# Two raw quads moved into an idle MLP buffer, with a newly searched instruction order, in a hand-ordered attention and MLP kernel

## The chip, the cores and the metric

One core of a Trainium2 chip. The metric is the device time of one execution in microseconds (us), median over timed runs; the four timed runs of the kernel before spread over 0.4% (358.04 to 359.32). Each profile is one further execution with its trace. "Half clock" below is a granted TensorE clock of 0.50 in the trace.

## The reference

```python
def phi(x):                                   # q, k, v: (8 batch, 8 heads, 576, 64); omega: (128, 64)
    proj = np.einsum('bhsd,md->bhsm', x, omega)
    return np.concatenate([np.cos(proj), np.sin(proj)], axis=-1) / np.sqrt(m)
q_p, k_p = phi(q), phi(k)
kv = np.einsum('bhsm,bhsd->bhmd', k_p, v);  z = np.sum(k_p, axis=2)
num = np.einsum('bhsm,bhmd->bhsd', q_p, kv);  den = np.einsum('bhsm,bhm->bhs', q_p, z)
x = (num / den) as (8, 576, 512)              # den kept away from 0
h = x.transpose(0, 2, 1) @ U @ V              # rank 32
u = x + h.transpose(0, 2, 1)
out = u + np.maximum(u @ w_ch1, 0.0) @ w_ch2  # 512 -> 2048 -> 512
```

The features are sines and cosines of random projections, so attention needs no score matrix. All matmuls run in bf16 with float32 sums.

## The kernel before

Every instruction of the kernel is a named word with its needs and buffers, and one long string, `ORDER`, says in which order the words are issued. Each engine runs its own words in that order: before, POOL issued `ld/q/2` at 13.03 us and `ld/k/3` at 15.61. The string was found by a search. The words of the argument, where a group `g` is a pair of heads ("head" in the prediction and below) and a quad `n` is two groups:

- `ld/k/n`, `ld/q/n`: load of a quad's keys or queries, issued by POOL (GpSimd). `ldv/n`: of its values. `low`: of the low-rank matrices V and U; `gate` clears their buffer first.
- `tpp/k/n`, `tp/k/n`: PE's transposes of the loaded quad, and their copy out of PSUM by DVE (VectorE).
- `ak/g`, `aq/g`: projections of keys and queries (64-row matmuls). `uk/g`, `uq/g`: DVE turns them into integer angles, 1.48 us and 1.21 us each.
- `s/c` (and `sk sq ck cq`): sine and cosine on ACT (ScalarE). `p` (`pk pq`): the quarter turn between them, on POOL.
- `kv/g`, `kvb/g`, `num/g`, `x/g`: key-value product (64 rows), its copy by DVE, the numerator, the division by DVE.
- `hu ut0 hn`: low-rank mixing. `w1 r w2 o st`: the MLP. `d/i`: a filler matmul on the identity. `@n`: the PSUM bank.

```python
    low_f = hidp.tile([P, NFT, SM], BF16, name="hid").rearrange("p f t -> p (f t)").bitcast(F32)
    Vf = low_f[:, 0:S]                          # the second of two hidden buffers stages V and U at first
    ...
    NRAW = 2                                    # two raw buffers for the quads' keys and queries
    def load(name, n):
        if ("raw", n) not in held:
            held["raw", n] = rawp.tile([P, 2, 2, NS * D], BF16, name="raw")
        return held["raw", n][:, "kq".index(name), :, :]
    ...
    need = [r for r in read_raw(name, n - NRAW)] if n >= NRAW else []
    add(("ld", name, n), POOL, lambda ...: nc.gpsimd.dma_start(load(name, n), quad(src, n)), needs=need)
    ...
    if n in BY_PE:                              # quads 0 to 3: transposed by PE
        add(key, PE, lambda ...: tp(key, blocks), needs=src + old + ["ident"], ...)
        add(done, on, lambda ...: ev(key, blocks, on), needs=[key], frees=[key])
    ...
    add(("uk", g), DVE, uk, needs=[("ak", g)] + slot, frees=[("ak", g)])
    add(("uq", g), DVE, uq, needs=[("aq", g), ("uk", g) if g else ("ukh", 0, 0)], frees=[("aq", g)])
```

So the third quad (`n = 2`) may be loaded only when the first quad's transposes have left its raw buffer.

Of the kernel before, what the change touches and what calls it, by code (L numbers as in the profile page):

```python
# [20 lines left out]
R = 32  # L21
# [14 lines left out]
begin first/k/0 first/k/1 ident first/q/0 om ld/k/0 d/0@5 warm d/1@1 ld/q/0 d/2@0 ld/k/1 d/3@7 d/4@5 ld/q/1 d/5@0 cast/k/1 cast/k/0 d/6@2  # L36
ldv/0 omb d/7@0 tpp/k/0/0@3 tpp/k/0/1@4 omt@7 tp/k/0/0 cast/q/0 WT tpp/k/0/2@0 tp/k/0/1 akh/0/0@5 tp/k/0/2 tpp/q/0/0@7 tpp/q/0/1@1 ukh/0/0
ld/k/2 tp/q/0/0 akh/0/1@2 tp/q/0/1 ukh/0/1 aq/0@4 d/8@6 gate skh/0/0 uq/0 d/9@7 low ak/1@0 skh/0/1 at/0@3 d/10@6 ut/0 pk/0 tpp/k/1@6 uk/1
sq/0 tpp/q/1@4 ck/0 ldv/1 pq/0 tp/k/1 d/11@1 aq/1@1 tp/q/1 ld/q/2 cq/0 uq/1 ak/2@3 wv/0 aq/2@6 uk/2 d/12@1 s/1 W1/0 ldv/2 kv/0/0@0 ld/k/3
uq/2 ak/3@2 W1/1 kv/0/1 p/1 uk/3 s/2 aq/3@6 kvb/0 tpp/k/2@2 uq/3 tpp/q/2@4 c/1 p/2 num/0 tp/k/2 tp/q/2 d/13@2 sk/3 x/0 ak/4@5 ld/q/3 wv/1  # L40
kv/1/0@3 c/2 uk/4 kv/1/1 pk/3 aq/4@1 kvb/1 kv/2/0@6 uq/4 sq/3 kv/2/1 lowc num/1 ck/3 kvb/2 kv/3/0@1 x/1 num/2 pq/3 kv/3/1 ld/k/4 hu0/0@0
cq/3 kvb/3 ut0x/0@3 huc0/0 hu0/1@4 ld/q/4 x/2 ut0/0 s/4 ut0x/1@0 W1/2 d/14@5 num/3 huc0/1 W1/3 ute0/0 hu0/2@7 ut0x/2@4 ut0/1 huc0/2
w1p/0/0@3 x/3 p/4 ut0/2 ute0/1 tpp/k/3@5 ute0/2 w1p/2/0@0 w1p/2/1 tp/k/3 hu0/3@7 w1p/1/0@2 w1p/3/0@1 huc0/3 ak/5@4 wv/2 c/4 w1p/3/1 uk/5
w1p/1/1 w1p/1/2 ut0x/3@7 ut0/3 w1p/3/2 w1p/2/2 w1p/0/1 ute0h/3 w1p/0/2 tpp/q/3@4 ute0/3 tp/4 w1/0/0 tp/q/3 aq/5@6 r/0/0 w1/0/1 w1/0/2 uq/5
w1/0/3 r/0/1 hn/0/0@4 r/0/2 w1/0/4@3 u/0/0 r/0/3 ldv/3 w1/0/5@0 r/0/4 s/5 ak/6@4 aq/6@1 w1/0/6@3 uk/6 w1/0/7@7 r/0/5 p/5 uq/6 r/0/6
w1/0/8@5 r/0/7 ak/7@0 r/0/8 aq/7@3 s/6 kv/4/0@6 uk/7 W2/0 w1/0/9@5 W2/1 kv/4/1 uq/7 W2/2 w1/0/10@2 r/0/9 p/6 c/5 hn/0/1@0 kvb/4 w1/0/11@5
u/0/1 num/4 wv/3 r/0/10 w1/0/12@4 x/4 r/0/11 w1/0/13@0 W2/3 r/0/12 d/15@1 kv/5/0@5 r/0/13 kv/5/1 s/7 ak/8@0 kvb/5 aq/8@3 w2/0/0/0@7 uk/8
num/5 c/6 p/7 uq/8 w1/0/14@0 w2/0/0/1 x/5 r/0/14 kv/6/0@1 ld/k/5 kv/6/1 c/7 ak/9@3 ld/q/5 w1/0/15@0 uk/9 ld/k/6 hnt/0@6 w2/0/0/2 ld/q/6
r/0/15 kvb/6 ut/tail/0 s/8 kv/7/0@3 kv/7/1 aq/9@5 num/6 kvb/7 num/7 x/6 p/8 w2/0/0/3 x/7 w2/0/1/0@0 w2/0/1/1 o/0/0 c/8 uq/9 w2/0/1/2 tp/5
hu/1@1 w2/0/1/3 s/9 huc/1 w2/0/2/0@7 o/0/1 hn/1/0@5 ldv/4 w2/0/2/1 p/9 st/0/0 u/1/0 hn/1/1@0 w2/0/2/2 u/1/1 w2/0/2/3 c/9 tu/1 w2/0/3/0@0  # L50
o/0/2 ak/10@2 ak/11@5 uk/10 w2/0/3/1 wv/4 tp/6 w2/0/3/2 uk/11 aq/10@3 w2/0/3/3 uq/10 kv/8/0@6 ldv/5 kv/8/1 kv/9/0@1 st/0/1 s/10 kvb/8
aq/11@4 kv/9/1 num/8 kvb/9 st/0/2 uq/11 w1/1/0@3 ldv/6 p/10 num/9 x/8 r/1/0 w1/1/1@4 s/11 o/0/3 w1/1/2@5 x/9 ld/k/7 w1/1/3@6 r/1/1 wv/5
w1/1/4@7 r/1/2 r/1/3 hnt/1@2 p/11 w1/1/5@0 r/1/4 ut/tail/1 c/10 ak/12@4 w1/1/6@1 uk/12 ld/q/7 w1/1/7@2 r/1/5 ld/k/8 r/1/6 ak/13@5 ld/q/8
r/1/7 kv/10/0@3 uk/13 aq/12@0 c/11 kv/10/1 w1/1/8@2 uq/12 w1/1/9@7 r/1/8 aq/13@5 kvb/10 tp/7 kv/11/0@0 r/1/9 uq/13 kv/11/1 s/12 num/10
w1/1/10@2 kvb/11 x/10 num/11 s/13 p/12 w1/1/11@5 x/11 tp/8 w1/1/12@3 w1/1/13@6 r/1/10 wv/6 r/1/11 hu/2@1 r/1/12 w1/1/14@0 r/1/13 huc/2
ld/k/9 c/12 w1/1/15@2 ld/q/9 hn/2/0@6 p/13 w2/1/0/0@3 u/2/0 r/1/14 hn/2/1@4 r/1/15 w2/1/0/1 u/2/1 c/13 ak/14@0 aq/14@6 w2/1/0/2 tu/2 uk/14
w2/1/0/3 uq/14 w2/1/1/0@0 o/1/0 kv/12/0@1 ldv/7 s/14 kv/12/1 ldv/8 kv/13/0@6 kvb/12 ak/15@3 st/0/3 kv/13/1 num/12 kvb/13 uk/15 tp/9 p/14
num/13 w2/1/1/1 x/12 w2/1/1/2 c/14 w2/1/1/3 x/13 wv/7 aq/15@1 ak/16@3 o/1/1 w1/2/0@6 uq/15 ld/k/10 w1/2/1@7 r/2/0 uk/16 ak/17@0 r/2/1
w1/2/2@6 s/15 uk/17 w1/2/3@5 w1/2/4@3 r/2/2 p/15 w1/2/5@2 r/2/3 r/2/4 hnt/2@0 w1/2/6@5 r/2/5 ut/tail/2 ld/q/10 aq/16@3 r/2/6 aq/17@6
kv/14/0@1 wv/8 c/15 kv/14/1 w1/2/7@5 kvb/14 uq/16 ld/k/11 num/14 w2/1/2/0@0 uq/17 s/16 w1/2/8@3 x/14 w2/1/2/1 tp/10 r/2/7 p/16 w1/2/9@4  # L60
r/2/8 kv/15/0@1 r/2/9 ak/18@5 st/1/0 kv/15/1 uk/18 aq/18@3 c/16 w2/1/2/2 ldv/9 w2/1/2/3 ldv/10 kvb/15 st/1/1 num/15 s/17 w1/2/10@7 x/15
w2/1/3/0@5 uq/18 r/2/10 w1/2/11@1 o/1/2 kv/16/0@6 r/2/11 ak/19@2 kv/16/1 s/18 st/1/2 wv/9 uk/19 aq/19@0 w2/1/3/1 ldv/11 w2/1/3/2 uq/19
wv/10 w1/2/12@4 kvb/16 ld/q/11 hu/3@2 r/2/12 ld/k/12 num/16 huc/3 w2/1/3/3 p/17 x/16 w1/2/13@1 hn/3/0@2 r/2/13 p/18 w2/2/0/0@7 u/3/0 c/17
w1/2/14@6 w1/2/15@0 r/2/14 hnt/3@1 hn/3/1@2 r/2/15 w2/2/0/1 s/19 u/3/1 w2/2/0/2 o/1/3 w2/2/0/3 ut/tail/3 c/18 st/1/3 p/19 w2/2/1/0@5 o/2/0
ak/20@0 st/2/0 kv/17/0@6 uk/20 w2/2/1/1 ld/q/12 c/19 tu/3 aq/20@3 kv/17/1 uq/20 ak/21@0 w2/2/1/2 kvb/17 w2/2/1/3 uk/21 tp/11 num/17
w2/2/2/0@4 x/17 s/20 w2/2/2/1 tp/12 o/2/1 kv/18/0@0 kv/18/1 aq/21@6 p/20 kv/19/0@2 kvb/18 kv/19/1 num/18 kvb/19 st/2/1 uq/21 w2/2/2/2
w2/2/2/3 x/18 s/21 num/19 ld/k/13 w1/3/0@0 x/19 w1/3/1@1 p/21 r/3/0 o/2/2 w1/3/2@7 r/3/1 ak/22@3 r/3/2 aq/22@1 ld/q/13 w1/3/3@0 uk/22 c/20
ld/k/14 w2/2/3/0@7 uq/22 w2/2/3/1 r/3/3 c/21 kv/20/0@5 ak/23@0 aq/23@3 kv/20/1 uk/23 w2/2/3/2 tp/13 s/22 w2/2/3/3 kvb/20 w1/3/4@0 o/2/3
uq/23 num/20 ldv/12 p/22 r/3/4 st/2/2 w1/3/5@7 hu/4@1 r/3/5 st/2/3 w1/3/6@3 huc/4 s/23 x/20 w1/3/7@2 w1/3/8@0 r/3/6 p/23 hnt/4@6 r/3/7
w1/3/9@5 ut/tail/4 r/3/8 w1/3/10@3 r/3/9 w1/3/11@0 wv/11 r/3/10 c/22 hn/4/0@6 ld/q/14 hn/4/1@2 u/4/0 w1/3/12@1 ld/k/15 ld/q/15 w1/3/13@4  # L70
u/4/1 r/3/11 wv/12 r/3/12 w1/3/14@7 r/3/13 tu/4 w1/3/15@6 r/3/14 ak/24@3 r/3/15 ak/25@0 uk/24 c/23 w2/3/0/0@7 tp/14 w2/3/0/1 uk/25
w2/3/0/2 kv/21/0@5 kv/21/1 aq/24@0 ak/26@2 kvb/21 w2/3/0/3 uq/24 num/21 o/3/0 w2/3/1/0@0 x/21 st/3/0 w2/3/1/1 uk/26 w2/3/1/2 w1/4/0@1
w1/4/1@5 r/4/0 aq/25@6 r/4/1 kv/22/0@1 uq/25 kv/23/0@3 s/24 kv/22/1 kv/23/1 w1/4/2@5 kvb/22 kvb/23 num/22 p/24 num/23 x/22 s/25 w2/3/1/3
x/23 w1/4/3@6 r/4/2 w1/4/4@7 p/25 o/3/1 r/4/3 hu/5@4 c/24 st/3/1 w2/3/2/0@2 huc/5 w2/3/2/1 r/4/4 aq/26@0 kv/24/0@3 kv/24/1 ak/27@5 kvb/24
w2/3/2/2 uq/26 w2/3/2/3 uk/27 w1/4/5@0 w1/4/6@1 o/3/2 r/4/5 num/24 r/4/6 w1/4/7@0 c/25 x/24 hn/5/0@1 hn/5/1@5 u/5/0 w1/4/8@4 r/4/7
w1/4/9@7 u/5/1 r/4/8 w2/3/3/0@0 r/4/9 tu/5 s/26 w2/3/3/1 aq/27@1 kv/25/0@3 uq/27 kv/25/1 ak/28@5 p/26 w2/3/3/2 st/3/2 kvb/25 s/27 uk/28
w1/4/10@2 ldv/13 w1/4/11@1 ldv/14 r/4/10 w1/4/12@7 p/27 r/4/11 num/25 r/4/12 w2/3/3/3 x/25 w1/4/13@2 o/3/3 w1/4/14@4 r/4/13 wv/13 c/26
w1/4/15@3 w2/4/0/0@7 ldv/15 st/3/3 w2/4/0/1 r/4/14 r/4/15 aq/28@5 tp/15 kv/26/0@0 uq/28 ak/29@2 kv/26/1 w2/4/0/2 uk/29 s/28 w2/4/0/3
w2/4/1/0@6 o/4/0 c/27 kvb/26 w1/5/0@2 p/28 st/4/0 w2/4/1/1 w1/5/1@7 r/5/0 c/28 hnt/5@3 w2/4/1/2 ut/tail/5 w2/4/1/3 r/5/1 w2/4/2/0@3 o/4/1
w1/5/2@2 num/26 r/5/2 w1/5/3@7 x/26 w2/4/2/1 r/5/3 w2/4/2/2 kv/27/0@0 ak/30@4 kv/27/1 uk/30 w2/4/2/3 w1/5/4@2 o/4/2 w1/5/5@5 kvb/27 r/5/4  # L80
w1/5/6@4 r/5/5 num/27 r/5/6 aq/29@2 x/27 ak/31@4 w2/4/3/0@7 uq/29 w2/4/3/1 w1/5/7@1 uk/31 w1/5/8@2 r/5/7 w1/5/9@5 r/5/8 s/29 w1/5/10@6
w1/5/11@1 w2/4/3/2 r/5/9 p/29 r/5/10 hu/6@0 r/5/11 w2/4/3/3 w1/5/12@2 o/4/3 wv/14 huc/6 w1/5/13@6 r/5/12 c/29 hn/6/0@0 hn/6/1@4 u/6/0
w1/5/14@7 w2/5/0/0@2 u/6/1 r/5/13 r/5/14 w1/5/15@0 tu/6 w2/5/0/1 r/5/15 kv/28/0@6 aq/30@4 aq/31@0 kv/28/1 w2/5/0/2 kvb/28 st/4/1 uq/30
w2/5/0/3 st/4/2 uq/31 w2/5/1/0@3 s/30 w2/5/1/1 st/4/3 w2/5/1/2 p/30 w2/5/1/3 num/28 w2/5/2/0@0 x/28 c/30 w2/5/2/1 o/5/0 w1/6/0@7 o/5/1
st/5/0 s/31 w2/5/2/2 st/5/1 w1/6/1@2 w1/6/2@5 r/6/0 p/31 r/6/1 w1/6/3@1 w1/6/4@2 wv/15 c/31 w2/5/2/3 w1/6/5@4 o/5/2 w1/6/6@3 st/5/2 r/6/2
# [57 lines left out]
def kernel(  # L143
# [125 lines left out]
    def load(name, n):  # L269
        if ("raw", n) not in held:  # L270
            held["raw", n] = rawp.tile([P, 2, 2, NS * D], BF16, name="raw")
        return held["raw", n][:, "kq".index(name), :, :]
# [427 lines left out]
```

## Time and profile before

| | |
|---|---|
| time, median | 358.24 us (358.04 to 359.32 over all runs beside the changed kernel) |
| the profiled execution | 360.0 us (its span 358.0), so 1.8 us over the median |
| PE (matmuls) busy | 95% of the span |
| half clock | 14.8 to 25.1 us, then full to the end |
| first head's num begins | 23.13 us |
| fourth head's num begins (the prediction's "mark") | 31.89 us |

The line numbers of one place differ by up to 4 between kernels, as the buffer lines push them down: the transposes are L321 before, L325 after, L324 in most experiments. Read PE's share first: what the kernel takes is a nearly gapless row of matmuls, plus what PE loses in the first 32 us. The prediction below shows the lines for that. The timeline columns are start, length, engine, line, operation and tiles; those of the busy time of each engine are stretch, its length, then PE, PEld, DVE, ACT, POOL, then clock, DMA share, GB/s.

```profile
8.31 0.71 POOL L298 DMA_DIRECT2D raw<-in_k_dram  x1 [3.48 <-PE ps L407]
```

```profile
23.13:31.89 8.76, 7.70 (x213) 6.03 (x211) 7.84 (x16) 7.57 (x6) 6.26 (x10) 0.89 0.78 122
```

The third quad's k load was issued at 8.31 us. From the first num to the mark DVE worked 7.84 us of 8.76: already then the fullest row, just ahead of PE (7.70).

### The profile page before, as it was taken

The page shows a single profiled execution, that of the slowest core. Times are in us where ns is not written, and L with a number is a line of the kernel's source. Part 1 is how long each engine was busy: PE and PEld are TensorE (multiplying, and loading weights), DVE is VectorE, ACT ScalarE, POOL GpSimd, SP SyncE. Part 2 cuts the span into 40 slices and gives each one's busy share as a digit, 9 for nine tenths or more (in the row PEclk, how much of TensorE's full clock was granted, in tenths as well). Part 3 has the DMA queues.
Part 4 walks back from the last instruction along what each step waited for, and adds up shares of the span by engine and source line. Part 5 has one row for each costly group of instructions (what it writes and reads, how often), then busy time and mean ns, then how long its engine had stood idle before and what let it go on. Part 6 is the DMA issues. An engine that isn't in the chain of part 4 may idle for free.

```text
span 358.0 us, 8213 instructions
## 1 busy us (share of the span) xinstructions
PE 341.3 (95%) x3544; PEld 180.4 (50%) x3585; DVE 193.2 (54%) x284; ACT 216.8 (61%) x223; POOL 117.3 (33%) x100
## 2 busy tenths in 40 slices
PE   7659999999999999989999999999999999999996
PEld 3446456454564554645455554554545544444444
DVE  3968868786687676866476754364320722000111
ACT  5868899559958877678829578437386004553210
POOL 5879185427634536324704043003230000000000
PEclk9869999999999999999999999999999999999999
DMA  8997989999999886999992086200722051511124
GB/s 173 224 239 116 203 142 195 217 178 227 192 194 192 123 246 128 115 177 166 196 183 46 3 212 140 62 3 0 148 60 44 2 104 29 117 31 29 37 53 88
DMA packets 68567, 45.06 MB, mean 126 GB/s; under 512 B 47156, under 2 KB 59828, under 8 KB 68532
## 3 DMA queue, kind: packets, MB, share of 16 engines
q1 hardware_dynamic: 55348, 30.09, 41.2%
q0 software_dynamic: 12816, 13.93, 25.5%
q8 instruction: 28, 0.46, 0.5%
q10 hardware_dynamic: 368, 0.52, 0.4%
q14 instruction: 7, 0.06, 0.1%
HBM read 37.16 MB, written 9.44 MB: 130 GB/s over the span
## 4 chain that ended last, share of the span: by engine, by line
PE 88%; DMA 7%; ACT 1%; issue 1%; POOL 1%; POOLq 0%
PE ps L610 35%; PE ps L630 34%; PE ps L430 5%; PE ps L444 4%; DMA raw<-in_q_dram 4%; DMA T<-raw 3%; PE ps L381 2%; PE ps L407 2%; PE ps L576 2%; PE ps L449 1%; PE ps L514 1%; ACT ft L416 1%; PE ps L321 1%; POOL ang L420 1%; PE ps L584 0%
## 5 line engine op out<-in xcount | busy, mean ns | idle before, releaser
L416 ACT ACTIVATE ft<-ang 128x2304 bf16<-128x2304 int16 (+2 forms) x67 | 134.1, 2020 | 35.4 <-DVE ang L359 15.3
L630 PE MATMUL ps<-W2b,hid 128*128 128x512 bf16 (+1 forms) x560 | 130.5, 373 | 2.6 <-issue 1.4
L623 ACT ACTIVATE hid<-ps 128x512 bf16<-128x512 f32 x144 | 81.9, 596 | 84.4 <-PE ps L610 83.9
L610 PE MATMUL ps<-uT,W1b 128*128 128x512 bf16 x512 | 121.7, 379 | 0.8 <-DMA uT<-u 0.6
L420 POOL TENSOR_SCALAR ang<-ang 128x2304 int32<-128x2304 int32 (+2 forms) x34 | 67.9, 2000 | 126.2 <-ACT ft L416 119.4
L359 DVE TENSOR_SCALAR ang<-ps 128x1280 int32<-128x1280 f32 (+2 forms) x66 | 84.8, 1313 | 24.7 <-PE ps L375 16.3
L630 PEld LDWEIGHTS <-hid 128*128 128x128 bf16 x592 | 55.4, 98 | 62.0 <-issue 2.1
L610 PEld LDWEIGHTS <-W1b 128*128 128x128 bf16 x576 | 54.3, 98 | 63.8 <-issue 1.4
L646 DVE TENSOR_TENSOR o<-ps,u 128x512 f32<-128x512 f32 x32 | 21.9, 686 | 52.1 <-PE ps L630 52.0
L430 PEld LDWEIGHTS <-ft 64*128 64x128 bf16 x1152 | 24.1, 96 | 9.9 <-issue 5.7
L430 PE MATMUL ps<-vq,ft 64*128 64x65 bf16 x1152 | 27.1, 193 | 1.4 <-DVE ang L359 0.9
L460 DVE TENSOR_TENSOR x<-ps,rec 128x640 bf16<-128x640 f32 x32 | 26.4, 825 | 1.1
L434 DVE CAST kvb<-ps 128x260 bf16<-128x260 f32 x32 | 13.4, 423 | 20.6 <-PE ps L430 19.8
L578 DVE TENSOR_TENSOR u<-ps,x 128x1024 bf16<-128x1024 f32 x16 | 19.2, 1221 | 9.6 <-PE ps L610 4.9
L305 POOL CAST vq<-vraw 128x1152 bf16<-128x1152 f32 x16 | 18.5, 1153 | 12.1 <-DMA vraw<-in_v_dram 12.1
L444 PEld LDWEIGHTS <-ft 128*128 128x128 bf16 x512 | 19.9, 99 | 5.0 <-issue 0.5
L444 PE MATMUL ps<-kvb,ft 128*128 128x65 bf16 x512 | 21.9, 195 | 0.0
L610 PE MATMUL ps<-utailT,W1b 128*128 128x512 bf16 x64 | 15.1, 379 | 0.0
L458 DVE RECIPROCAL ps<-ps 128x10 f32<-128x10 f32 x32 | 7.2, 224 | 13.8 <-PE ps L449 13.3
L381 PE MATMUL ps<-WT,T 64*128 64x128 bf16 x256 | 13.5, 222 | 1.1 <-DMA T<-raw 0.6
L298 POOL DMA_DIRECT2D raw<-in_k_dram x15 | 10.9, 725 | 10.2 <-ACT hid L623 6.3
L407 PE MATMUL ps<-T,WT 64*128 64x512 bf16 x64 | 13.2, 387 | 0.0
(58 smaller groups left out, 150.7 us busy)
## 6 DMA issues: line engine op xcount, KB each, us to landing
out_dram<-o SPq DMA_DIRECT2D x70, 128.0 KB, 2.4
vraw<-in_v_dram SPq DMA_DIRECT2D x15, 576.0 KB, 5.7
raw<-in_k_dram POOLq DMA_DIRECT2D x15, 288.0 KB, 5.7
raw<-in_q_dram POOLq DMA_DIRECT2D x15, 288.0 KB, 6.0
W1b<-in_moe_w_ch_dram POOLq DMA_DIRECT2D x4, 512.0 KB, 9.9
W2b<-in_moe_w_ch_dram POOLq DMA_DIRECT2D x4, 512.0 KB, 8.9
vraw<-in_v_dram POOLq DMA_DIRECT2D x1, 576.0 KB, 7.5
ang<-in_q_dram ACTq DMA_DIRECT2D x1, 288.0 KB, 3.5
```

Source lines behind the costliest of these rows:

```text
L359: nc.vector.tensor_scalar(out=dst, in0=src, scalar1=TO_UNITS, scalar2=None, op0=ALU.mult)
L381: nc.tensor.matmul(pk[:, e, i * P:(i + 1) * P], kT[r, c, :], WT[r, :])
L407: nc.tensor.matmul(pq[:, e, :], WT[r, :], transposed("q", n)[r, c:c + 4, :])
L416: nc.scalar.activation(out=held["ft", g].rearrange("p f a c -> p f (a c)")[:, f, lo:hi], in_=low[:, lo:hi, 0], func=ACT.Sin, scale=TO_RAD)
L420: nc.gpsimd.tensor_scalar(out=ang, in0=ang, scalar1=TURN / 4.0, scalar2=1.0, op0=ALU.add, op1=ALU.mult)
L430: nc.tensor.matmul(kv_ps[:, hh, o], ft[r, f, 0, c:c + M], vq[n % NV][r, NS * (g % 2) + s, :], start=(s == 0), stop=(s == NS - 1))
L444: nc.tensor.matmul(nd[:, hh, t, :], ft[:, f, 1, c:c + P], kvb[:, hh, f, :], start=(f == 0), stop=(f == 1))
L460: nc.vector.tensor_tensor(out=x[:, :, hp * P:(hp + 1) * P].rearrange("p t (h d) -> p h t d", h=2), in0=nd[:, :, :, 0:D], in1=rec.unsqueeze ...
L610: nc.tensor.matmul(one(key), W1b[:, f // 4, ct, f % 4 * P:(f % 4 + 1) * P], uT[:, :, ct, :], start=(ct == 0), stop=(ct == NCT - 1))
L623: nc.scalar.activation(out=held["hid", b][:, f, :], in_=one(at_bank), func=ACT.Relu)
L630: nc.tensor.matmul(one(key)[:, 0:cs.stop - cs.start], held["hid", b][:, f, t * P:(t + 1) * P], W2b[:, f, cs], start=(f == 0), stop=(f == N ...
L646: nc.vector.tensor_tensor(out=held["o", b, t][:, cs], in0=one(key)[:, 0:cs.stop - cs.start], in1=u[:, t, cs], op=ALU.add)
```

## The change

The intent is to take away the wait of the third and fourth quads' loads for the raw buffers, and to let a new search use that. (1) The first two quads' raw data go into the unused rest of the second hidden buffer, so quads 2 and 3 find both raw buffers free. (2) The whole `ORDER` is searched anew, first with a raised price on changes between 64-row and full-height matmuls, then without the raise.

```diff
-    low_f = hidp.tile([P, NFT, SM], BF16, name="hid").rearrange("p f t -> p (f t)").bitcast(F32)
+    low_h = hidp.tile([P, NFT, SM], BF16, name="hid").rearrange("p f t -> p (f t)")
+    low_f = low_h.bitcast(F32)
+    early_raw = [low_h[:, 2 * (S + NS * R) + n * 4 * NS * D:2 * (S + NS * R) + (n + 1) * 4 * NS * D].rearrange(...)
+                 for n in range(2)]
...
-            held["raw", n] = rawp.tile([P, 2, 2, NS * D], BF16, name="raw")
+            held["raw", n] = early_raw[n] if n < 2 else rawp.tile([P, 2, 2, NS * D], BF16, name="raw")
...
-                need = [r for r in read_raw(name, n - NRAW)] if n >= NRAW else []
+                need = [r for x in "kq" for r in read_raw(x, n - NRAW)] if n >= NRAW + 2 else []
...   (the first relu of the second batch also waits for the readers of quads 0 and 1)
 ORDER, cut to the first 30 us and to the words of the argument ("." is other words)
-... ukh/0/0 ld/k/2 . pk/0 . pq/0 . ld/q/2 . ld/k/3 . tpp/k/2@2 uq/3 tpp/q/2@4 . num/0 . uk/4 . uq/4 . num/3
+... ldv/0 . pk/0 . ak/1@2 ld/k/2 tp/q/1 aq/1@6 ck/0 ld/q/2 uk/1 ld/k/3 pq/0 . tpp/k/2@3 . num/0 . uq/3 . uk/4
+... . uk/5 . uq/4 . uq/5 . num/3
...   (all later words in another order too)
```

## The prediction

> **What bounds the kernel now.** I read the page's busy table and slices first, then the chain that ended last in order of time, then who PE (TensorE's matmuls) waited for, then the timeline of the first 30 us. The page:
>
> ```profile
> PE 341.3 (95%) x3544; PEld 180.4 (50%) x3585; DVE 193.2 (54%) x284; ACT 216.8 (61%) x223; POOL 117.3 (33%) x100
> PEclk9869999999999999999999999999999999999999
> DMA  8997989999999886999992086200722051511124
> PE 88%; DMA 7%; ACT 1%; issue 1%; POOL 1%; POOLq 0%
> ```
>
> PE is 95% busy and 88% of the chain that ended last. The other engines stand at 61% or less. So most of the span is a gapless row of matmuls, and an order of instructions can win only what PE loses between them. The exception is the first tenth: the clock row has a 6 in its third slice (17.9 to 26.8 us), and the DMA row starts 8, 9, 9.
>
> Whom PE waited for (us in total, times, longest):
>
> ```profile
> PE ps L321 <- DMA raw<-in_q_dram: 3.6, 3, 2.6
> PE ps L228 <- DVE ang L359: 1.5, 2, 1.0
> PE ps L430 <- DVE ang L359: 0.9, 1, 0.9
> PE ps L321 <- DVE ang L359: 0.8, 1, 0.8
> PE ps L610 <- DMA uT<-u: 0.6, 1, 0.6
> PE ps L381 <- DMA T<-raw: 0.6, 1, 0.6
> ```
>
> By the timeline all of these but the last two fall before 28 us. The last two are at 155.3 and 158.6 us, together 1.2 us: DMA transposes that landed late. So PE loses time in three places: the start, those two waits, and something that no wait shows, the change between 64-row matmuls (L381, L407, L430: keys, queries and kv of the attention) and full-height ones. It is read from the chain, where the same group appears with two lengths:
>
> ```profile
> 90.08 0.58 PE ps L430 x36
> 90.66 0.61 PE ps L444 x16
> 91.28 0.13 PE ps L449 x4
> 91.40 0.86 PE ps L610 x4
> 92.27 0.51 PE ps L444 x16
> ...
> 56.91 0.68 PE ps L430 x36
> ...
> 57.93 0.97 PE ps L610 x4
> ```
>
> Sixteen L444 take 0.51 us after full-height work and 0.61 after 64-row work; four L610 take 0.86 or 0.97; thirty-six L430 take 0.58 behind other 64-row work (the queries, L407, stand before 90.08) and 0.68 behind full-height work. So one change costs about 0.10 us, in either direction.
>
> The start, from the chain's early part:
>
> ```profile
> 13.03 8.91 DMA raw<-in_q_dram
> 21.99 1.14 PE ps L321 x9
> 23.13 0.88 PE ps L444 x16
> 24.27 3.29 ACT ft L416 x2
> ```
>
> The query load of the third quad was issued by POOL at 13.03 and landed at 21.94. PE's transposes of it stand before the num of the first head pair (L444; a head is a pair of heads from here on), and ScalarE's next sine waits for that num because it needs its feature buffer. So a late load stopped PE for 2.6 us and ScalarE for 2.9 us.
>
> [...] 0.50 of the clock from 15 to 25 us, 1.00 before and after; nine transposes took 1.14 us there against 0.50 later. [...] with V, U and two v loads on the SP queue the q load took 8.9 us against a median of 6.0.
>
> **The change, part by part.** Neither list of operations nor any shape changes. The same 3585 matmuls are issued, 20 of them fillers in both.
>
> 1. Buffers. The first two raw quads go into the second hidden buffer, idle until the second batch's first relu. In the built program the third quad's k load loses its waits for earlier loads, PE, DVE and ScalarE, and the fourth quad's loads likewise. On POOL the order is now quarter turn, k2, q2, k3, where it was k2, two quarter turns, q2, cast of v, W1, k3. Each load costs POOL 0.72 us to issue, each quarter turn 1.0 to 2.1. With the first quarter turn at about 9.7, as before, q2 is issued at about 11.5, not 13.03, and k3 at about 12.2, not 15.61. The wait of PE for q2 (2.6 us) and of ScalarE (2.9) should go.
>
> 2. But that does not shift the end by 2.6 us, because the next thing in the start binds. I take as mark the num of the fourth head, after which PE never starves: it began at 31.89. It needs that head's last cosines, those need the last quarter turn on POOL, which before ended at 29.7. POOL's work in the new order from 9.7: quarter turns 1.04, 1.26, 2.1, 2.1, 1.25, 1.03; three loads 2.2 and one more 0.73; two W1 loads 1.55; three v casts 3.5; the low-rank casts 1.93. Sum 18.7, so 28.4 if gapless. POOL must also wait for the second head's sine (ready at about 17.1 when POOL is at 16.2): 0.9. That gives 29.3. Cosine 1.1, so num at about 30.6: 1.3 us earlier. Against it: V, U and v1 are now loaded about 3.5 us earlier (the zeroing that releases them moved ahead on DVE) and compete with q1, which landed at 10.15 and which PE now needs before the second head's keys. If it slips by 1.5 us, the mark slips to about 31.7 and the gain is gone. I take 0.9 as mean.
>
> 3. Changes of mode. Counting the PE words of both lists: 109 changes before, 97 after; from the mark on 90 and 83. Seven at 0.10 on a gapless PE: 0.7 us. The other five lie in the start, where PE waits anyway, and are worth little.
>
> 4. Work moved across the mark. The sixth head's keys and queries are now ahead of it (0.33 + 0.22), one low-rank product and its Vb product behind it (0.13 + 0.22). Net 0.2 us less after the mark. Fillers: one behind the mark in both; those at the very end run beside the last store.
>
> 5. The two late transposes, 1.2 us. In the new order the fourth batch's transpose has as much full PE work ahead of its use as before (9.6 us by adding durations), but the eight quad loads near it no longer straddle it. New thin places: the first head of the fifth quad is used 7 us after its transpose can start (14.5 before; that transpose took 8.3 us), W1's last quarter is loaded some 10 us later, about 8 us ahead of its use (it took 9.7), and the sixth batch's transpose has 7.4 us instead of 15. I expect these to cost on average what the old ones did: 0.
>
> Sum: 0.9 + 0.7 + 0.2 + 0 = 1.8 us, so 358.2 - 1.8 = 356.4.
>
> **Rivals.** (a) The start gives its full 2.6 to 2.9 us because other waits shrink with it: 354.5. For it: the wait for q2 is the longest of PE's, and DVE is gapless from 8 to 20 us, then idle for 2.8. Against: POOL's sum in step 2. (b) The start gains nothing, because DMA is saturated there (the row of nines): loads issued earlier merely wait in the queue, and q1 comes later. Then only steps 3 and 4 remain: 357.3. For it: the DMA row's 8, 9, 9 over the first 27 us. (c) A new late transpose or weight load: each costs 0.6 to 2 us at one place; with two of them 358 to 359. For: the thin places in step 5, and transposes of 8.3, 10.9 and 11.1 us when loads crossed them. (d) PE stays at half clock longer: the grant came back at 25.05, just before the gapless part. [...]
>
> **Range and chances.** The sure part (3 and 4) is 0.9. The start adds 0 to 2.5, new waits take 0 to 2 and may give back up to 1.2. So 354.2 to 358.4 should hold it 8 times in 10. Faster by over 2% means under 351.0, 7 us: all waits of PE in the list above, with its shorter rows, are 10 to 11 us together, so nearly all would have to go; 0.02. Slower by over 2% means over 365.4: several new waits of 3 us; 0.02. Within 2%: 0.96.
>
> **What would show it.** Step 1: k2, q2, k3 issued back to back before 13 us and no wait of PE for raw in the third quad over 0.5 us; wrong if q2 lands after 20. Step 2: last quarter turn ending near 29.3, the mark near 30.9. Step 3: the same groups with the same two lengths (0.51 and 0.61), seven fewer of the longer; wrong if one change costs other than 0.10. Step 5: PE's waits after the mark sum to about 1.2; a larger sum with W1b, uT or T as releaser is rival (c). Rival (d): the 0.50 clock lasts beyond 25 us.

## The result, and the profile after

| | before | after |
|---|---|---|
| time, median | 358.24 | 361.41 (361.04 to 362.16, 4 runs) |
| ratio of fast runs | | 1.0085 (95%: 1.0058 to 1.0112) |
| third quad's k load: issued, landed | 8.31, 13.69 | 10.98, 19.65 |
| third quad's q load | 13.03, 21.94 | 11.70, 21.91 |
| V load | 9.07, 18.05 | 5.81, 16.64 |
| first head's num begins | 23.13 | 21.27 |
| mark begins | 31.89 | 34.66 |
| the second batch's mixing begins (`hn/1/1`), all work ahead of it done | 68.90 | 71.92 |
| changes of matmul mode up to there / after it | 41 / 68 | 30 / 67 |

Ratios here are the mean time of one kernel's fast runs over that of the other's in the same rounds, so not quite the ratio of the medians quoted. The change is 0.9% slower, clear of the noise, where 0.5% faster had been predicted. The first num and the mark are given as they stand in the chain; PE's own record of their first matmul starts some 0.2 us earlier. The changes of mode are counted with the low-rank products `hu` (32 columns) as a mode of their own, as the prediction did, though what a change to or from `hu` costs was not measured; 64-row work against all other work gives 32 / 56 before and 24 / 56 after.

The page after, busy times, clock and the shares of the chain:

```profile
PE 343.9 (96%) x3548; PEld 183.3 (51%) x3585; DVE 194.3 (54%) x284; ACT 217.2 (60%) x223; POOL 117.0 (33%) x100
...
PEclk9856999999999999999999999999999999999999
...
PE 91%; DMA 4%; DVE 2%; issue 1%; ACT 1%; POOL 0%; POOLq 0%; DVEq 0%
```

PE is busier by 2.6 us for the same matmuls. The clock row has a 5 and a 6 where before had one 6. In the chain the DMA share fell from 7% to 4%, and DVE, which did not appear before, has 2%.

Whom PE waited for, after:

```profile
PE ps L325 <- DMA raw<-in_k_dram: 2.2, 1, 2.2
PE ps L385 <- DVE ang L363: 1.5, 2, 0.9
...
PE ps L434 <- POOL vq L309: 1.1, 1, 1.1
PE ps L378 <- DVE ang L363: 1.0, 1, 1.0
```

The wait for the q load is gone, as intended. One of nearly the same length for the k load stands in its place, and below it are new waits for DVE (L363 is `uk` and `uq`). The chain of waits in the start:

```profile
10.98 8.68 DMA raw<-in_k_dram
...
19.70 1.14 PE ps L325 x9
...
21.27 0.88 PE ps L448 x16
...
28.76 2.62 DVE ang L363 x2
...
31.42 1.17 PE ps L434 x36
...
34.66 0.88 PE ps L448 x16
```

Read it from the bottom: the mark (34.66) comes behind the fourth head's kv (L434, both halves), this behind 2.62 us of DVE's `uk/5` and `uq/4` (by the order, that kv takes the PSUM bank 6 that `uq/4` frees), and DVE's row goes back to the transposes of the third quad (L325) and so to the k load. POOL's quarter turns, in which the prediction saw the bound, do not stand between the k load and the mark. DVE's and POOL's timelines after:

```profile
20.88 0.76 DVE L329 COPY T<-ps 128x1152 bf16<-128x1152 bf16 x1 [2.08 <-PE ps L325]
...
28.76 2.61 DVE L363 TENSOR_SCALAR ang<-ps 128x1280 int32<-128x1280 f32 x2
...
31.82 1.21 DVE L363 TENSOR_SCALAR ang<-ps 128x1024 int32<-128x1024 f32 x1
32.95 0.42 DVE L438 CAST kvb<-ps 128x260 bf16<-128x260 f32 x1
```

```profile
28.68 1.03 POOL L424 TENSOR_SCALAR ang<-ang 128x1024 int32<-128x1024 int32 x1
```

DVE stood idle for 2.08 us until the transposes came, then from 24.0 to 33.4 us it had no gap. In that row lie `uk/5` and `uq/5`, the sixth head's, ahead of the fourth head's `kvb` (32.95), which the mark needs. POOL's last quarter turn ended at 29.71, about where it ended before (29.68), five microseconds ahead of the mark. The busy times from the first num to the mark, and from 29 to 36 us:

```profile
21.27:34.66 13.39, 11.26 (x223) 9.21 (x221) 11.62 (x20) 9.55 (x7) 12.23 (x14) 0.63 0.96 190
```

```profile
29.00:36.00 7.00, 6.48 (x140) 5.57 (x139) 5.59 (x9) 3.18 (x2) 5.72 (x6) 0.52 0.86 145
```

Between the first num and the mark DVE now does 11.62 us of work where it did 7.84, that is 3.8 more. By the order it has three words more in that stretch: `uq/3` (behind the first num now, ahead of it before), `uk/5` and `uq/5`, 1.21 + 1.48 + 1.21 = 3.9 us. I put most of the longer stretch, 13.39 us instead of 8.76, down to it; e5 below, without `uk/5` and `uq/5` there, has 11.52. POOL is fuller too (12.23), but the last of its words that the mark needs is the quarter turn that ended at 29.71. PE ran at half clock here (28.9 to 35.7), so its 6.48 us of "busy" are slow, not full: sixteen L448 took 0.88 us at 34.66, at half clock, and 0.51 at 53.46, at full clock.

### The profile page after: what moved, and what is told of

The parts are those of the page before. It is cut to its first block, busy times and chain, and to the rows that moved or that the text cites.

```text
span 359.9 us, 8227 instructions
## 1 busy us (share of the span) xinstructions
PE 343.9 (96%) x3548; PEld 183.3 (51%) x3585; DVE 194.3 (54%) x284; ACT 217.2 (60%) x223; POOL 117.0 (33%) x100
## 4 chain that ended last, share of the span: by engine, by line
PE 91%; DMA 4%; DVE 2%; issue 1%; ACT 1%; POOL 0%; POOLq 0%; DVEq 0%
PE ps L614 35%; PE ps L634 34%; PE ps L434 5%; PE ps L448 5%; DMA raw<-in_k_dram 2%; PE ps L411 2%; PE ps L385 2%; PE ps L580 2%; DMA hid<-in_k_dram 1%; PE ps L453 1%; PE ps L325 1%; DVE ang L363 1%; PE ps L518 1%; PE ps L232 1%; PE ps L588 0%
## 5 line engine op out<-in xcount | busy, mean ns | idle before, releaser
L614 PE MATMUL ps<-uT,W1b 128*128 128x512 bf16 x512 | 119.7, 379 | 0.1
L363 DVE TENSOR_SCALAR ang<-ps 128x1280 int32<-128x1280 f32 (+2 forms) x66 | 85.4, 1316 | 20.2 <-PE ps L379 13.9
L434 PE MATMUL ps<-vq,ft 64*128 64x65 bf16 x1152 | 26.6, 197 | 2.5 <-POOL vq L309 1.1
L434 PEld LDWEIGHTS <-ft 64*128 64x128 bf16 x1152 | 23.8, 99 | 9.8 <-issue 5.5
L448 PEld LDWEIGHTS <-ft 128*128 128x128 bf16 x512 | 21.0, 101 | 5.8 <-issue 0.7
L448 PE MATMUL ps<-kvb,ft 128*128 128x65 bf16 x512 | 22.6, 198 | 0.0
L438 DVE CAST kvb<-ps 128x260 bf16<-128x260 f32 x32 | 13.5, 424 | 12.2 <-PE ps L434 11.9
L309 POOL CAST vq<-vraw 128x1152 bf16<-128x1152 f32 x16 | 18.3, 1152 | 2.9 <-DMA vraw<-in_v_dram 2.8
L572 DVE CAST hu<-ps 128x512 bf16<-128x512 f32 x7 | 4.8, 692 | 13.5 <-PE ps L518 13.5
```

What stands on the lines that cost most here:

```text
L363: nc.vector.tensor_scalar(out=dst, in0=src, scalar1=TO_UNITS, scalar2=None, op0=ALU.mult)
L434: nc.tensor.matmul(kv_ps[:, hh, o], ft[r, f, 0, c:c + M], vq[n % NV][r, NS * (g % 2) + s, :], start=(s == 0), stop=(s == NS - 1))
L448: nc.tensor.matmul(nd[:, hh, t, :], ft[:, f, 1, c:c + P], kvb[:, hh, f, :], start=(f == 0), stop=(f == 1))
L614: nc.tensor.matmul(one(key), W1b[:, f // 4, ct, f % 4 * P:(f % 4 + 1) * P], uT[:, :, ct, :], start=(ct == 0), stop=(ct == NCT - 1))
```

## The experiments

The theory after reading both traces was: the loss lies in the first 70 us; the late k load starts it, and DVE's longer row or the second stretch of half clock carries it to the mark. Rivals: the new buffers themselves, the rest of the order, the earlier V and U loads, the clock alone.

### 1. Which part: buffers, order, start, rest

```diff
 e1: the old ORDER in the changed kernel                e2: the new ORDER in the kernel before
 e3: old ORDER up to hn/1/1, new behind it              e4: new ORDER up to hn/1/1, old behind it
```

> The old order with the new buffers alone. Theory 'order': the buffers change no wait that sets the end, so within 0.7 us of the kernel before (358.2). Theory 'buffers': if the earlier issue of the third quad's k load (it no longer waits for the first quad's readers) crowds out the loads that PE waits for, 360 or more; if it helps, 356 or less.

> The new order with the old buffers. In the new order the third and fourth quads' loads stand behind all readers of the first two raw buffers, so theory 'order' says the old buffers cost nothing and the time is that of the changed kernel, 361.4 within 0.7. If the buffers are needed by the new order, it is slower: 363 or more.

> The old order up to the second batch's Vb product (68.9 us in the old trace), the new order from there; both orders have done the same work at that point. Theory 'start': the traces put +3.0 us before this point and -1.1 after it, so this kernel should take 358.2 - 1.1 = 357.1. Rival 'spread' (the loss comes from the whole new order, for example from transposes and loads that collide): 359 or more.

> The opposite splice: the new order up to the same point, the old order from there. Theory 'start': 361.4 + 1.1 = 362.5. Rival 'spread': at most 360.

| | median us | ratio to before (95%) |
|---|---|---|
| buffers alone | 357.44 | 0.9974 (0.9944 to 1.0005) |
| order alone | 361.40 | 1.0096 (1.0063 to 1.0129) |
| old start, new rest | 358.36 | 1.0004 (0.9975 to 1.0033) |
| new start, old rest | 361.56 | 1.0094 (1.0068 to 1.0120) |

The buffers, which e3 and e4 have too, cost nothing. The whole loss comes with the new order, and from the first 70 us of it. The rest is worth nothing in either direction: from the first weight load of `hn/1/1` to the MLP's last one the traces of the new order, of both splices and of the old order with the new buffers take 283.6 to 284.0 us. Only the profiled run of before takes 285.0, with its two late transposes (1.2 us). The other traces of the same rest (e1, e4, e9, e12 and e17) show no wait for a DMA there. They were a feature of that one execution, which was also 1.8 us over its kernel's timed runs. The expectation of a gain for the third kernel had been read off it, and fell, as did the 362.5 for the fourth.

### 2. Was it DVE's extra work before the mark, or V and U loaded earlier?

```diff
 e5:  . x/1 -ak/5@3 . -uk/5 . -aq/5@4 . -uq/5 . num/3 . ut0x/3 +ak/5@3 ut0/2 +uk/5 . +aq/5@1 . +uq/5 . w1p/2/1
 e6:  omt@2 -gate d/9 -low . ukh/0/1 +gate +low ldv/1
 e8:  both
```

> The new order with the sixth head's keys and queries (two projections on PE, two scalings on DVE of 1.48 and 1.21 us) moved back behind the fourth head, where the old order had them; four changes of matmul mode more. Theory 'DVE order': these 2.7 us stand on a gapless DVE ahead of the fourth head's kv copy and num, so the mark comes about 2 us earlier and the kernel takes 361.4 - 2 + 0.4 = 359.8. Theory 'clock': the second stretch of half clock makes the loss and comes anyway: 361.4 to 361.8. Theory 'loads': same as clock.

> The new order with the zeroing that releases the V, U and second v loads moved back behind the first head's second scaling, as in the old order. Theory 'loads': the third quad's k load no longer shares the DMA engines with them, lands 2 us or more earlier, PE's wait of 2.2 us for it goes, and the kernel takes 359 to 360. Theories 'clock' and 'DVE order': the wait shrinks but the mark stays within 0.7 us, 361.4.

> Both edits, the late sixth head and the late zeroing. If loss is the sum of DVE order and loads: 358 to 358.5, as the old order. If the clock makes it: 361 or more with the second stretch of half clock still there. If undoing both also lets the clock recover once and for all at 25 us, the three theories are one chain.

Measured: with the sixth head behind the fourth 363.38 (1.0143, 1.0125 to 1.0160); with V and U later 360.80 (1.0073, 1.0044 to 1.0103); with both 362.65 (1.0136, 1.0101 to 1.0170), though there the profiled run had its mark's weight load as early as 30.3. The second shows that the earlier V and U loads are not the main cause: most of the loss stayed, and in its trace, with V landing a microsecond later, the k load still landed at 19.70. They do not leave that load alone, though. In the trace of both edits, whose order is the same up to there, it landed at 17.36. And over all traces a third quad's k load issued at 4.8 us landed at 12.5 to 13.3 where the loads of V, U and the second v began at 8.7 to 9.7 us (e1, e3, e10, e12, e17), and at 17.3 to 17.5 where they began at 5.7 to 5.8 (e11, e14). Which of these loads does it is not shown. The first is a miss that teaches something. The mark did come 1.6 us earlier, yet the end came 2 us later, and its trace has new waits of PE: 1.8 us of a kv (L433) for `x`, 1.1 of the mixing (L579) for `uk` or `uq`, 0.7 of a key projection (L384) for `u`. I take it that the displaced `uk/5` and `uq/5` now stood ahead of these. Bringing the mark forward by pushing DVE's work past it is no gain; this kernel is not an undo of that part of the change, since the old order has other words around it.

### 3. Was it the half clock?

```diff
 e7:   15 fillers: 2 ahead of ak/3, 3 of kv/0/0, 4 of tpp/k/2, 2 each of ak/5, kv/2/0, kv/3/0 (banks picked from all)
 e13:  10 fillers in banks that are free there: 3 (@0) ahead of ak/5, 3 (@0) of kv/2/0, 4 (@3) of kv/3/0
```

> The new order with 15 fillers put where PE waits anyway between 13 and 31 us. Theory 'clock': the records show full clock from 5 us on, or at least from 25 on, [...] and the kernel takes 359 to 360. Theory 'DVE order': with DVE gapless until the fourth head's kv copy, a faster PE gives at most 1 us: 360.4 to 361.4.

> The new order with 10 fillers in PSUM banks that are free, where PE waits between 26 and 31 us. Theory 'clock by itself': the stretch at half clock that begins near 29 us goes, or shortens, and the kernel takes about 360 ([...] from the runs of the new order at a mean clock of 0.976 and 0.981). Theory 'clock follows': DVE's row, not PE's rate, sets the fourth head's num, and the time stays 361.4 within 0.6 or grows by what fillers cost.

The first try, 365.28 (1.0194, 1.0171 to 1.0217), failed as an experiment: the fillers waited for their own PSUM banks, up to 1.65 us, and the clock fell anyway (a mean of 0.979 over its runs, as in the changed kernel). The second did what it should: 360.84 (1.0063, 1.0040 to 1.0086), with the clock at 1.00 through the stretch:

```profile
29.00:36.00 7.00, 6.45 (x156) 4.59 (x155) 6.86 (x14) 3.18 (x2) 5.28 (x6) 1.00 0.90 151
```

Here DVE is busy 6.86 of 7.00 us: with PE fast again, DVE still fills the stretch. The mark came only 0.3 us earlier, and the median is 0.57 us below the changed kernel's; the intervals of the two ratios overlap, so this is not clear of noise. So the second half-clock stretch by itself costs about 0.6 us of the 3.2. Whether it follows from PE waiting is not shown. The first stretch (15.9 to 26.1 us in this trace) was still there, so the clock of the whole start is not tested by this.

### 4. Was it the late k load?

```diff
 e9:   new ORDER up to kvb/0 (18.4 us), old behind it      e10: old ORDER up to there, new behind it
 e11:  new ORDER:  ldv/0 +ld/k/2 +ld/q/2 d/6@4 . ak/1@2 -ld/k/2 . ck/0 -ld/q/2 uk/1
 e14:  new ORDER:  ldv/0 +ld/k/2 d/6@4 . ak/1@2 -ld/k/2 tp/q/1
```

> The new order up to the first head's kv copy on DVE (18.4 us in both traces), the old order from there. It keeps the later k load of the third quad and drops the early sixth head. Theory 'loads first' (the late k load alone makes the loss): 360.5 to 361.5. Theory 'middle' (the loss is made between 18 and 40 us, by DVE's order and the PSUM banks that the early sixth head holds): 358 to 359.

> The opposite: the old order up to the same point, the new one from there. Theory 'middle': 360.5 to 361.5, with a mark (fourth head's num) 2 us or more later than the old order's. Theory 'loads first': 358 to 359.

> The new order, but the third quad's k and q loads issued right behind the first v load (near 4.8 and 5.5 us, which the new buffers allow) and not behind the first quarter turn (10.98 and 11.70). PE's 2.2 us wait for that k load should go in every theory. Theory 'loads first': 359 to 359.5. Theory 'middle': DVE, gapless from 24 us on, starts its row up to 2 us earlier, so 359.5 to 361; and if V, U and v land later because of it, no gain.

> The new order with the third quad's k load alone issued behind the first v load; its q load stays behind the quarter turn. If the k load makes the loss, as with both loads early: 358.7 within 0.7. If the q load does: 361 or more. If each makes half: 360.

| | median us | ratio to before (95%) | k load landed | first num | to the mark | mark |
|---|---|---|---|---|---|---|
| before | 358.24 | | 13.69 | 23.13 | 8.76 | 31.89 |
| after | 361.41 | 1.0085 | 19.65 | 21.27 | 13.39 | 34.66 |
| e9, new first 18 us | 359.03 | 1.0026 (0.9979 to 1.0072) | 19.55 | 23.01 | 8.77 | 31.78 |
| e10, old first 18 us | 360.07 | 1.0040 (1.0014 to 1.0067) | 13.14 | 19.85 | 12.98 | 32.83 |
| e11, k and q loads early | 358.74 | 1.0000 (0.9973 to 1.0028) | 17.30 | 19.31 | 12.65 | 31.96 |
| e14, k load alone early | 358.30 | 1.0005 (0.9977 to 1.0033) | 17.48 | 19.38 | 12.63 | 32.01 |

The last row is the test that settles it: one word moved, a load that POOL issues at 4.80 us instead of 10.98, and the changed kernel is back at the time before, 3.1 us faster. It is not quite the old place of the word, which was issued at 8.31 there, but the load lands after the old one did (17.48 against 13.69), so the order isn't favoured by it. PE's wait for this load is gone, and with it half clock in both stretches: 15.0 to 18.4 and 28.7 to 32.1 us are left of 15.2 to 25.5 and 28.9 to 35.7. The timed runs agree: their mean granted clock is 0.979 for the changed kernel and 0.988 for e14. So part of the 3.1 us may come by way of the clock; how much, no run separates. That the place of this one load sets it going is shown either way. Its chain and its busy times from the first num to the mark:

```profile
19.38 0.63 PE ps L447 x16
...
32.01 0.59 PE ps L447 x16
```

```profile
19.38:32.01 12.63, 9.01 (x223) 7.62 (x223) 11.73 (x20) 10.40 (x8) 12.61 (x15) 0.87 0.89 194
```

The table also shows why the order lost so much by it. With the new order behind 18 us, the way from the first num to the mark takes 12.6 to 13.4 us, with DVE busy 11.5 to 11.7 us of it; with the old order 8.8. The search put the sixth head's angles and `uq/3` there, 3.9 us of DVE's work, and for the mark to stay the first num had to come 3.9 us sooner, at about 19.3. The k load's landing at 19.65 and the nine transposes behind it made that impossible: the num came at 21.27. Under the old rest (e9) the same late k load is nearly free, since the num stands behind the q load there too, which landed at 21.8 (21.9 before). The times show this interplay (a ratio of 1.0026 for the late load under the old rest, 1.0085 under the new); that DVE's row makes it is read from the traces. The fourth row (e10) keeps 1.4 us of the loss though its k load landed early: its first num comes 0.5 us later than e14's, because PE's transposes of the k load wait 0.8 us for DVE (`uk/3`), and its way to the mark is 0.35 us longer. That this makes the whole of its 1.4 us I did not test.

The columns add up to the result. Median time less mark is 326.4 before, 326.8 after, 326.3 for e14, 326.8 for e11, and 327.2 for e9 and e10. Only the two kernels of part 2 whose displaced work lies behind their mark are off: e5 (363.38 - 33.08 = 330.3), and e8 by still more.

### 5. What does a change of mode cost?

```diff
 e15, old ORDER: +20 fillers, each between two 64-row words (40 more changes)
 e16, old ORDER: +20 fillers, each between two full-height words (no more changes)
```

> The old order with 20 fillers of 0.216 us, each between two words of 64-row matmuls while PE is gapless (70 to 250 us): 40 changes of mode more. With 0.10 us a change: 358.2 + 4.3 + 4.0 = 366.5. If a change costs nothing in a gapless row: 362.5.

> The control: the same 20 fillers, each between two full-height words near the same places, no change of mode more: 358.2 + 4.3 = 362.5 in either theory. The difference between the two kernels over 40 is the cost of one change.

The first gave 366.92 (1.0246, 1.0220 to 1.0271), 8.58 us over before. Twenty fillers at 0.216 us are 4.32; the other 4.26 over 40 changes are 0.106 us each (0.09 to 0.14 by the interval; one filler also waited 0.3 us for its bank). Its chain shows one filler (L229) between two halves of a kv product:

```profile
90.41 0.29 PE ps L431 x18
90.70 0.32 PE ps L229
91.02 0.39 PE ps L431 x18
91.41 0.61 PE ps L445 x16
```

The filler takes 0.32 behind 64-row work, and the half behind it 0.39 against 0.29. The control was spoiled: 368.66 (1.0286, 1.0257 to 1.0314), where 362.5 was expected. In its trace six of the added fillers waited for their PSUM bank, 4.0 us in all (two fillers that before has too make the rest of this row); the other 2 us stay open:

```profile
PE ps L229 <- DVE ang L360: 5.4, 8, 1.0
```

So the difference between the two kernels says nothing. That the unhampered fillers of the control took 0.216 us by the trace, and 0.32 in the other, says what it was built to say.

### 6. A kernel that beats both

The old order is short from the first num to the mark, and its num waits for the q load. The new buffers allow that load at once:

```diff
 old ORDER in the changed kernel (e12; e17 is the same again):
-ukh/0/0 ld/k/2 tp/q/0/0 . aq/1@1 tp/q/1 ld/q/2 cq/0
+ukh/0/0 ld/k/2 ld/q/2 tp/q/0/0 . aq/1@1 tp/q/1 cq/0
```

> The old order with the new buffers, and the third quad's q load issued right behind its k load (near 5.5 us) and not at 13. That is what the buffers were for. The waits of PE (2.6 us) and ScalarE (2.9) for that load should go. If the start's next bound is POOL's quarter turns as the prediction had it, the gain is about 1 us: 357. If V, U and v, pushed back, become the next wait, 358 or more.

> The old order with the new buffers and the third quad's q load right behind its k load, once more, five rounds. If the gain of the first run is real: about 356.5 us, a ratio of 0.995 with an interval below 1. If it was a matter of clock phase and chip: a ratio of 0.998 to 1.002.

The first time 356.83 (0.9982, 0.9924 to 1.0040), with one of four runs slow, so it was run again with more rounds: 356.30 (355.31 to 356.95), ratio 0.9949 (0.9925 to 0.9972). That is 0.5% faster than before, and 356.30 / 361.41 = 0.986 of the changed kernel's median, from another call. The q load was issued at 5.50 and landed at 13.99; PE no longer waits for it. The chain of the second run:

```profile
19.77 0.88 PE ps L447 x16
...
28.77 0.51 PE ps L447 x16
```

First num 3.4 us earlier than before, way to the mark 9.00, mark 3.1 us earlier; of this 1.9 reached the median. Some of the difference is chance between executions: this profiled run, with 355.31 us, is the fastest of the six. Two more things have a part that no run separates: the new buffers alone (e1, 0.9974; the intervals overlap), and the clock, which was at half for 18.3 to 21.7 us here and not at all in the start of e12's trace, where before had 14.8 to 25.1.

## Why the prediction was wrong

**Step 1, the loads: here it failed.** The issue times were right: q2 at 11.70 (11.5 predicted), k3 at 12.41 (12.2). It also read rightly from the order that POOL now has the quarter turn ahead of the k load. But it followed only the load for which PE had waited, and never worked out what the new place does to k2: issued 2.7 us later, landed 6.0 us later, as the load took 8.7 us instead of 5.4. The DMA row was full meanwhile: the DMA column of the stretches gives 1.14 from 10.98 to 19.66 us, and 1.03 before from 8.31 to 13.69. PE's wait of 2.6 us for q was replaced by one of 2.2 us for k, and q2 landed at 21.91, past the 20 us that the prediction named as its own sign of failure. The risk that it did name, q1 slipping behind V, U and v1, did not come: q1 landed at 10.19 (10.15 before). Moving that one word (e14) gives back 3.1 us, the whole loss.

**Step 2, the mark: right sum, wrong engine.** The last quarter turn ended at 29.71, 0.4 off the predicted 29.3. But the mark came at 34.66, not 30.6 to 30.9. Even with the k load early it is 32.01, which I put down to DVE's row, with 3.9 us more up to there. Step 4 had seen the sixth head's projections ahead of the mark and charged PE's 0.55 us for them (0.11 short, as it left out L374 and L375); it did not charge DVE's 2.7 us for their angles. Of the miss at the mark, 34.66 - 30.9 = 3.8 us, the k load makes 2.65 (34.66 - 32.01). I put the other 1.1 down to DVE's row; no run takes that row alone out.

**Step 3, changes of mode: size right, place wrong.** A change costs 0.106 us by measurement (0.10 predicted), and the groups have the same two lengths after as before:

```profile
51.58 0.58 PE ps L434 x36
...
53.46 0.51 PE ps L448 x16
...
56.69 0.68 PE ps L434 x36
...
57.70 0.97 PE ps L614 x4
```

Of the 12 changes saved, five lie before the mark, six between it and `hn/1/1`, one behind. Between the mark and `hn/1/1` PE was busy 36.70 us of 37.01 before and 36.17 of 37.26 after: 0.5 us less work, and 0.8 more idle, in two waits for DVE (`x` and the copy of `uT`; 0.5 and 0.3 us). So the predicted saving was made on PE and then waited away, where the prediction had PE never starve after the mark.

**Step 4** moved 0.2 us and is too small to see in any run.

**Step 5, the late transposes.** No new ones came, so rival (c) fell. The two old ones were gone too, but nothing was gained, as they were not in the typical run: five other traces of the same rest show none. Step 5 itself counted 0 for them, which was right; only the range had room for the 1.2 us.

**Rivals.** (a) is refuted, as the start gave nothing. (b), loads issued earlier merely queue up, was right for q2 (issued 1.3 us earlier, landed at the same time), but as an end time (357.3) it missed the late k2. (d), half clock longer, came true: half clock again from 28.9 to 35.7 us, whose removal was worth about 0.6 us (e13, not clear of noise). Whether it is cause or consequence of the late mark stays open in part.

**The sum.** 361.41 - 356.4 = 5.0 us. The mark makes 3.8 of it. The rest is what steps 3 and 4 took off behind the mark (0.9) and which did not come, and about 0.3 more that no run resolves.

## What to carry to other kernels

When an order frees one load from its wait, look up where every other load now stands in the issue order: with the DMA row full (1.14 in its column) a load issued 2.7 us later landed 6 us later here, and one word's place was worth 0.9%. Nor did an earlier issue come back in full: the same 288 KB landed 2.2 us earlier (e14) when issued 6.2 us earlier than after. I put the later mark down to a row that had not set it before (DVE's, 11.62 us of work in 13.39), so add up every engine's work up to it, those that did not wait before too. And compare a profiled execution with its own kernel's timed runs before counting an odd wait in it as something to win. Fillers placed with no free PSUM bank in view waited up to 1.65 us and cost 3.9 us (e7, 365.28 against 361.41); ten in free banks gained 0.6 (e13), not clear of noise.
